# A spectral mixing kernel: first combination of units 3 and 5 on VectorE, butterflies of unit 2 on TensorE, halved inverse products of unit 5, a new order of the program

## The chip, the cores and the metric

The kernel runs on one core of one Trainium2 chip, in float32. The time is the device time of one execution in microseconds (us); the median of three runs is quoted. The profile comes from one further execution, traced by the hardware profiler.

## The reference, cut to what matters

```python
# x: 1 x 2048 x 512 (sequence L by channels D); all outputs are summed into one array
g = sigmoid((x * gate_w).sum(-1, keepdims=True))
a = irfft2(rfft2(x) * (w_r + 1j * w_i))          # two-dimensional Fourier filter
# K[d, l] = 2 Re sum_n C[d, n] exp(A[d, n] dt[d] l)
b = irfft(rfft(x, 2 * L) * rfft(K, 2 * L))[:L] + x * D_skip
return g * a + (1 - g) * b
```

For the inputs drawn here every step `dt` is so small that the kernel `K` is constant along the sequence, so `b` is a scaled prefix sum of `x` plus a scaled `x`. The kernel counts on the chip for how many channels this holds and has a general branch behind an `If` at the end, which is not entered.

## The kernel before

The two-dimensional transform is done by matrix products with constant tables. It has five stages.

1. **First products.** `x` (4 MB) arrives in ten parts. A part is multiplied on TensorE by a small table (`C_`, L276), in two halves `u`: one half takes the difference of the part's two blocks straight from `x`, as two accumulating products; the other takes their sum, which GpSimd forms first (`fold`, L259). VectorE transposes each product into the array `AR` (`c_a`, L284).
2. **Eight units.** A unit is a group of frequencies. Per unit: products along the sequence (`P_`, L435), a copy out of PSUM on ScalarE (`t_a`, L440), products along the channels (`D_`, L453), butterflies that combine the four parts of each product (`Z_`, L470 to L473, four VectorE instructions in PSUM, ahead of which ScalarE copies two parts aside in `d_a`, L462), and two products with the filter `w` on VectorE (`W` and `U`, both `W_`, L490), which leave `tw`. For the units in the list `ZPE` the butterflies are done by TensorE instead, as eight more products with the table `zfw` (L457) accumulated into `D_`, and `d_a` and `Z_` are not issued. Units 1 and 7 go through all this in two halves of 64 frequencies each (numbered 11, 21 and 17, 27).
3. **Combination.** GpSimd adds and subtracts in two steps of two instructions each: `p_a` (L496, L497, `px` from `tw`) and `g_a` (L509, L510, `gt` from `px`). ScalarE then mends one row (`h_a`, L517, L518).
4. **Inverse products** along the channels on TensorE (`I_`, L537, into `p_v`), a copy of half of it on ScalarE (`i_a`, L543), and an add and a subtract on VectorE into `AI` (`V_`, L551).
5. **The end.** Frequency 0 gets a product of its own (`K_`, L557) and a copy (L559). Then eight products with the last table but one (`B_`, L571), transposed by VectorE (`b_a`, L575), and eight output tiles (`Q_`, L597), each added to the other branch's result by VectorE (`last_a`, L610; L607 for the tile `LASTQ`, which leaves in two halves) and stored.

Beside this runs the other branch: copies to PSUM (`x_a`, L335), four prefix sums on VectorE (`scan`, L338), scalings on ScalarE (L342, L347), an adding transfer on GpSimd's queue (`both`, L352), the gate (L375, L385) and its products on GpSimd (`damp`, L370). The gate also scales the last table (`gated`, L587 on VectorE, L588 on ScalarE, from a copy of the gate in PSUM, `near`, L366).

Each engine works through its instructions in the order in which the program issues them. That order is written by hand in the string `PLAN`: a word is a letter for a step and the number of a unit, a part or a tile (`p5` is `p_a` of unit 5). PSUM has four buffers for all steps; a step that needs one waits until an earlier holder is released. Intermediates share thirteen SBUF buffers (`blk`), the filters and the last table four.

Of the kernel before, what the change touches and what calls it, by code (L numbers as in the profile page):

```python
# [15 lines left out]
P = 128  # L16
# [7 lines left out]
ZPE = (3, 5)  # L24
LASTQ = 7
LASTC = 7
FIRSTB = 0
# [4 lines left out]
R7 R0 C1 F2 J0 C0 c1 c0 T0 C2 c2 F3 C3 c3 F4 C4 J1 F5 R1 C5 F6 F8 F9 c4 c5 C6 c6 C8 R9 C9 c8 c9 R6 F7 N1 C7 c7 P11 l1  # L32
P21 l4 t11 t21 N0 N3 D11 d11 D21 d21 Z11 Z21 P17 P27 N4 N2 t17 L1 U11 R5 W11 U21 D17 t27 d17 P4 t4 Z17 l7 W21 L7 U17
X1 D27 p11 g11 d27 h11 Z27 D4 p21 g21 L4 P6 l0 d4 W17 U27 Z4 W27 p17 P0 U4 R4 g17 p27 W4 X3 X0 g27 t6 h21 P2 L0 t0 p4
D6 x1 t2 l6 h17 m1 G4 d6 h27 L6 G5 y1 k0 R8 X2 Z6 g4 U6 W6 k1 o3 o2 R10 D0 k2 k3 l2 d0 h4 l5 G1 x2 Z0 W0 D2 U0 L2 d2
l3 P3 P5 o4 G2 r1 p6 O0 t3 m2 y2 I11 S1 D3 g6 Z2 i11 p0 g0 W2 U2 o5 S0 r2 h6 L5 L3 O1 p2 t5 V11 I17 i17 x0 I6 h0 U3 o0
g2 V17 I21 i21 W3 D5 i6 S2 m0 y0 p3 g3 h2 V21 V6 O2 I0 o1 W5 I27 r0 U5 p5 g5 i0 i27 h3 x3 H2 o6 V0 I4 i4 V27 m3 I2 V4
i2 V2 h5 I3 I5 i3 V3 S3 u0 O3 i5 H4 E0 K0 V5 K1 B0 y3 E1 B3 b0 b3 B1 B4 B2 b1 B7 b2 B6 H5 o7 b4 r3 b7 Q1 Q0 u1 b6 B5
H1 E3 E2 Q3 H0 b5 H3 Q4 q1 q0 H7 H6 q3 Q2 q2 q4 Q6 q6 Q5 Q7 q5 q7
"""  # L40
SPLIT = [int(w[2:]) for w in PLAN.split() if w[0] == "P" and w[1] == "1" and len(w) == 3]
FOLDS = [0, 0, 1, 1, 1, 1, 1, 1, 1, 1]
ORDER = [8, 9, 0, 1, 10, 2, 11, 3, 12, 4, 13, 5, 14, 6, 15, 7, 16]
# [138 lines left out]
def body(ctx: ExitStack, tc: tile.TileContext, x, xg, xt, w, wh, prms, vecs, gw,  # L182
# [49 lines left out]
    t_ = {}  # L232

    with tc.manual_schedule():
# [20 lines left out]
        def fold(q, E):  # L255
            n = 64 * (PARTS[q].stop - PARTS[q].start)
            f = t_["f", q] = blk([P, 2, 512], "f")
            xv = xin(q)
            E.tensor_tensor(f[:, 0, :n], xv[:, 0], xv[:, 1], op=ALU.add)  # L259
            if FOLDS[q] == 2:  # L260
                E.tensor_tensor(f[:, 1, :n], xv[:, 0], xv[:, 1], op=ALU.subtract)


        def C_(q):
            n = 32 * (PARTS[q].stop - PARTS[q].start)
            p = t_["c", q] = [psum("p_s1") for _ in range(2)] if q == LASTC else [psum("p_s1")] * 2
            tiles = [(g, h, slice(64 * h, 64 * h + 64)) for g in range(2) for h in range(2)]
            if FOLDS[q] == 2:
                for g, h, r in tiles:
                    T.matmul(p[0][64 * g:64 * g + 64, h, :2 * n], s1e[r, 0:64], t_["f", q][r, :, g * n:g * n + n], start=True, stop=True, tile_position=(64 * h, 64 * g))  # L270
            else:
                for u in range(1, -1, -1):
                    for i in range(1 if FOLDS[q] > u else 2):
                        for g, h, r in tiles:
                            src = t_["f", q][r, 0] if FOLDS[q] > u else xin(q)[r, i]
                            T.matmul(p[u][64 * g:64 * g + 64, h, u * n:u * n + n], s1e[r, 64 * u * i:64 * u * i + 64], src[:, g * n:g * n + n], start=i == 0, stop=i == 1 or FOLDS[q] > u, tile_position=(64 * h, 64 * g))  # L276

        def c_a(q):
            k = PARTS[q]
            n = 32 * (k.stop - k.start)  # L280
            av = AR.rearrange("p u c (h t) d -> p u h t c d", h=2)
            for u in range(1, -1, -1):
                pv = t_["c", q][u][:, :, :2 * n].rearrange("p h (u t c d) -> p u h t c d", u=2, c=16, d=2)
                V.transpose(av[:, u, :, k], pv[:, u])  # L284
# [33 lines left out]

        def new(key, make):
            if key not in t_:  # L320
                t_[key] = make()
            return t_[key]
# [169 lines left out]
        def p_a(n):  # L492
            u, r, vs = unit(n)
            t1, t2 = (cut(t_["t", u, k], n).rearrange("p (o i) k -> p o i k", o=2) for k in range(2))
            po = new(("px", u), lambda: blk([P, 2, 2, 2, P], "px")).rearrange("p x a o k -> p x o a k")[..., r]
            G.tensor_tensor(po[:, 0], t1[:, :, 0:4:2], t1[:, :, 1:4:2][:, :, ::-1], op=ALU.subtract)  # L496
            G.tensor_tensor(po[:, 1, :, ::-1], t2[:, :, 0:4:2], t2[:, :, 1:4:2][:, :, ::-1], op=ALU.add)  # L497
# [101 lines left out]
        def last_a(j, E, p):  # L599
# [4 lines left out]
            if j == LASTQ:  # L604
                for f in range(2):
                    o_ = o[:, 512 * f:512 * f + 512]
                    E.tensor_tensor(o_.rearrange("p (e c b) -> p e c b", e=2, b=4), p[f].rearrange("p b (e c) -> p e c b", e=2), xv[..., 4 * f:4 * f + 4], op=ALU.add)  # L607
                    (nc.sync, nc.scalar)[f].dma_start(out[j, :, 512 * f:512 * f + 512], o_)
            else:
                E.tensor_tensor(o.rearrange("p (e c b) -> p e c b", e=2, b=8), p.rearrange("p b (e c) -> p e c b", e=2), xv, op=ALU.add)  # L610
                nc.sync.dma_start(out[j], o)

        def a_a(j):
# [18 lines left out]
            "f": lambda q: fold(q, V), "F": lambda q: fold(q, G), "C": C_, "c": c_a, "N": lambda k: N_[k](),  # L632
# [257 lines left out]
```

## Time and profile before

| | |
|---|---|
| three runs | 110.46, 110.65, 110.81 us, median 110.65 |
| the profiled execution's own time | 110.1 us |
| its span | 108.3 us |
| TensorE (PE) busy | 93.2 us, 86% |
| VectorE (DVE) busy | 85.3 us, 79% |
| GpSimd (POOL) busy | 75.5 us, 70% |
| ScalarE (ACT) busy | 51.5 us, 48% |
| granted TensorE clock, mean | 0.987 |
| moved by DMA | 27.67 MB |

The span runs from the first to the last recorded work; 1.8 us of the execution's own time lie around it. Shares are averages over five stages with different limits, so a busy engine of the table need not be the one that sets the end. PE and PEld are TensorE's products and its weight loads, which overlap. In the views, an entry in square brackets behind an instruction is the time its engine had stood idle before it, and what ended the wait.

### The profile page before, as it was taken

The page shows a single profiled execution, that of the slowest core. Times are in us where ns is not written, and L with a number is a line of the kernel's source. Part 1 is how long each engine was busy: PE and PEld are TensorE (multiplying, and loading weights), DVE is VectorE, ACT ScalarE, POOL GpSimd, SP SyncE. Part 2 cuts the span into 40 slices and gives each one's busy share as a digit, 9 for nine tenths or more (in the row PEclk, how much of TensorE's full clock was granted, in tenths as well). Part 3 has the DMA queues.
Part 4 walks back from the last instruction along what each step waited for, and adds up shares of the span by engine and source line. Part 5 has one row for each costly group of instructions (what it writes and reads, how often), then busy time and mean ns, then how long its engine had stood idle before and what let it go on. Part 6 is the DMA issues. An engine that isn't in the chain of part 4 may idle for free. (4 is left out here: it accounts for less than half of the span.)

```text
span 108.3 us, 2285 instructions
## 1 busy us (share of the span) xinstructions
PE 93.2 (86%) x872; PEld 77.6 (72%) x872; DVE 85.3 (79%) x134; ACT 51.5 (48%) x89; POOL 75.5 (70%) x70
## 2 busy tenths in 40 slices
PE   6899976999997999989899999976699999999200
PEld 6797753999797945368799999966243869999100
DVE  0248989579799788999999999996889979788500
ACT  0000005455749399999796996946870170000000
POOL 0059853222999998599999999999999999700000
PEclk9999999999999999999999999999999999999995
DMA  3999999999999991099978993998325950779950
GB/s 65 373 366 404 397 389 344 382 422 417 427 405 410 417 395 80 0 200 225 191 242 197 254 250 123 273 229 163 95 98 98 189 106 3 312 297 360 393 214 13
DMA packets 8560, 27.67 MB, mean 255 GB/s; under 512 B 968, under 2 KB 1352, under 8 KB 8028
## 3 DMA queue, kind: packets, MB, share of 16 engines
q1 hardware_dynamic: 7132, 22.86, 57.0%
q0 software_dynamic: 1088, 4.19, 20.2%
q10 hardware_dynamic: 320, 0.38, 1.0%
q8 instruction: 9, 0.15, 0.6%
q14 instruction: 11, 0.09, 0.2%
HBM read 19.01 MB, written 4.21 MB: 214 GB/s over the span
## 5 line engine op out<-in xcount | busy, mean ns | idle before, releaser
L490 DVE TENSOR_TENSOR tw<-p_d,w 128x1024 f32<-128x1024 f32 (+1 forms) x20 | 19.3, 1005 | 1.1 <-ACT w L411 0.5
L370 POOL TENSOR_TENSOR XT<-XT,gb 128x1024 f32<-128x1024 f32 x8 | 19.3, 2552 | 0.2 <-DMA XT<-v 0.2
L435 PE MATMUL p_t<-s2e,AR 128*128 128x128 f32 x128 | 16.7, 285 | 2.1 <-DVE AR L284 0.9
L435 PEld LDWEIGHTS p_t<-s2e,AR 128*128 128x128 f32 x128 | 15.7, 196 | 3.4 <-DVE AR L284 1.3
L453 PE MATMUL p_d<-et,dfw 128*128 128x256 f32 (+1 forms) x80 | 16.8, 343 | 0.8 <-ACT v L347 0.3
L537 PE MATMUL p_v<-dbw,gt 128*128 128x128 f32 x128 | 15.2, 276 | 1.6 <-ACT gt L518 1.6
L597 PEld LDWEIGHTS p_oa<-s1a,AR 128*128 128x128 f32 x128 | 15.2, 196 | 1.7 <-ACT s1a L588 0.9
L537 PEld LDWEIGHTS p_v<-dbw,gt 128*128 128x128 f32 x128 | 14.7, 192 | 1.9 <-ACT gt L518 1.8
L597 PE MATMUL p_oa<-s1a,AR 128*128 128x128 f32 x128 | 15.6, 283 | 0.0
L453 PEld LDWEIGHTS p_d<-et,dfw 128*128 128x128 f32 x80 | 12.0, 191 | 3.5 <-ACT gt L517 1.1
L259 POOL TENSOR_TENSOR f<-AI 128x512 f32<-128x512 f32 (+1 forms) x8 | 9.0, 1140 | 7.8 <-DMA AI<-in_x_dram 7.8
L496 POOL TENSOR_TENSOR px<-tw 128x512 f32<-128x512 f32 (+1 forms) x10 | 11.8, 1184 | 2.2 <-DVE tw L490 2.2
L284 DVE STREAM_TRANSPOSE AR<-p_s 128x512 f32<-128x512 f32 (+1 forms) x20 | 10.8, 589 | 2.9 <-PE p_s L276 2.8
L497 POOL TENSOR_TENSOR px<-tw 128x512 f32<-128x512 f32 (+1 forms) x10 | 11.8, 1180 | 0.0
L551 DVE TENSOR_TENSOR AI<-p_v,po 128x512 f32<-128x512 f32 (+1 forms) x20 | 10.4, 577 | 1.3 <-ACT po L543 1.3
L440 ACT COPY et<-p_t 128x1024 f32<-128x1024 f32 (+1 forms) x10 | 8.4, 836 | 6.0 <-PE p_t L435 6.0
L509 POOL TENSOR_TENSOR gt<-px 128x512 f32<-128x512 f32 (+1 forms) x10 | 10.6, 1063 | 0.8
L276 PE MATMUL p_s<-AI,last 64*64 64x128 f32 (+1 forms) x192 | 10.2, 347 | 1.0 <-DMA AI<-in_x_dram 1.0
L510 POOL TENSOR_TENSOR gt<-px 128x512 f32<-128x512 f32 (+1 forms) x10 | 10.6, 1060 | 0.0
L575 DVE STREAM_TRANSPOSE AR<-p_ia 128x1024 f32<-128x1024 f32 x8 | 9.4, 1222 | 1.4 <-PE p_ia L571 1.4
L338 DVE TENSOR_TENSOR_SCAN p_x<-p_x,XT 128x1024 f32<-128x1024 f32 x4 | 9.2, 2293 | 1.3 <-ACT p_x L335 1.3
L610 DVE TENSOR_TENSOR AI<-p_oa,XT 128x1024 f32<-128x1024 f32 x7 | 8.2, 1211 | 1.5 <-PE p_oa L597 1.5
(67 smaller groups left out, 123.0 us busy)
## 6 DMA issues: line engine op xcount, KB each, us to landing
w<-in_w_dram SPq DMA_DIRECT2D x8, 512.0 KB, 7.7
XT<-in_xt_dram SPq DMA_DIRECT2D x4, 1024.0 KB, 8.9
XT<-v POOLq DMA_DIRECT2D x4, 1024.0 KB, 9.9
out_dram<-AI SPq DMA_DIRECT2D x7, 512.0 KB, 3.4
AI<-in_x_dram SPq DMA_DIRECT2D x6, 512.0 KB, 7.7
gb<-gd SPq DMA_DIRECT2D x4, 512.0 KB, 5.2
AI<-in_x_dram SPq DMA_DIRECT2D x4, 256.0 KB, 3.2
s1a<-in_c_s1a_dram SPq DMA_DIRECT2D x4, 256.0 KB, 4.4
```

The source lines that it names most:

```text
L284: V.transpose(av[:, u, :, k], pv[:, u])
L370: E.tensor_tensor(r, r, t_["gb", h % 2], op=ALU.mult)
L435: T.matmul(cut(p, n, v)[:, 2 * q:2 * q + 2], AR[:, q % 2, 8 * (q // 2) + u, :, v], s2e[:, 2 * u + v], start=True, stop=True)
L453: T.matmul(d[:, o, 1:3] if h else d[:, o, 0:4:3], dfw[:, 2 * h + o], e[:, 2 * h + o], start=True, stop=not z)
L490: E.tensor_tensor(t, z, w, op=ALU.mult)
L496: G.tensor_tensor(po[:, 0], t1[:, :, 0:4:2], t1[:, :, 1:4:2][:, :, ::-1], op=ALU.subtract)
L497: G.tensor_tensor(po[:, 1, :, ::-1], t2[:, :, 0:4:2], t2[:, :, 1:4:2][:, :, ::-1], op=ALU.add)
L509: G.tensor_tensor(gv[:, :, 0], src[0], src[1], op=ALU.subtract)
L510: G.tensor_tensor(gv[:, ::-1, 1], src[0], src[1], op=ALU.add)
L537: T.matmul(p[:, v - vs[0], h, o], rows(u, o, v, h), dbw[:, h, o], start=True, stop=True)
L551: V.tensor_tensor(ai[:, :, :, k], t_["pi", n][:, 0:len(vs), :, 0], t_["po", u][:, v], op=ALU.subtract if k else ALU.add)
L597: T.matmul((p[b // 4][:, b % 4] if j == LASTQ else p[:, b]).rearrange("p (e c) -> p e c", e=2), VA[:, i, 8 * (k % 2) + b, :, k // 2], s1a[ ...
```

## The change

- `PDVE`: `p_a` of units 3 and 5 (four instructions) is issued on VectorE instead of GpSimd. Both inputs and the output are in SBUF.
- `ZPE` gets unit 2: its butterflies become eight more TensorE products, and its `d_a` and `Z_` go.
- Unit 5's inverse products, copy and `V_` are issued in two halves (words `I15`, `i15`, `V15`, `I25`, `i25`, `V25`); the matrix products are the same.
- The two halves `u` of the first products and of their transposes become words of their own (`C`, `c` for the half without a fold, `j`, `w` for the folded one), so that the last part's unfolded half can be issued earlier.
- The tile that leaves in two halves is 4 instead of 7. `LASTROWS` holds one slice with all rows, and the new value of `FIRSTB` and the new word `v` change nothing in the program.
- `PLAN` is a new order. The units come as 1, 7, 4, 0, 6, 5, 3, 2; before, as 1, 7, 4, 6, 0, 2, 3, 5.

```diff
-ZPE = (3, 5)
-LASTQ = 7
-LASTC = 7
-FIRSTB = 0
+ZPE = (2, 3, 5)
+LASTQ = 4
+FIRSTB = 1
...
-g2 V17 I21 i21 W3 D5 i6 S2 m0 y0 p3 g3 h2 V21 V6 O2 I0 o1 W5 I27 r0 U5 p5 g5 i0 i27 h3 x3 H2 o6 V0 I4 i4 V27 m3 I2 V4
...
+o0 p0 D3 o1 W5 S1 g0 y0 o4 h4 p6 I17 O2 U5 U3 g6 p5 i17 W3 I27 p3 S3 h0 i27 V17 L2 D2 r0 g5 U2 h5 V27 W2 I0 o5 i0 I4
...
+APART = (7,)
+LASTROWS = [slice(0, P)]
+PDVE = (3, 5)
...
-        def fold(q, E):
+        def fold(q, u, op, E):
             n = 64 * (PARTS[q].stop - PARTS[q].start)
-            f = t_["f", q] = blk([P, 2, 512], "f")
+            f = new(("f", q), lambda: blk([P, 2, 512], "f"))
             xv = xin(q)
-            E.tensor_tensor(f[:, 0, :n], xv[:, 0], xv[:, 1], op=ALU.add)
...
+            E.tensor_tensor(f[:, u, :n], xv[:, 0], xv[:, 1], op=op)
...
-        def C_(q):
+        def C_(q, u):
             n = 32 * (PARTS[q].stop - PARTS[q].start)
...
+            p = new(("c", q, u if q in APART else 0), lambda: psum("p_s1"))
+            for i in range(1 if FOLDS[q] > u else 2):
+                for g in range(2):
+                    for h in range(2):
+                        r = slice(64 * h, 64 * h + 64)
+                        src = t_["f", q][r, u] if FOLDS[q] > u else xin(q)[r, i]
+                        T.matmul(p[64 * g:64 * g + 64, h, u * n:u * n + n], s1e[r, 64 * u * i:64 * u * i + 64], src[:, g * n:g * n + n], start=i == 0, stop=i == 1 or FOLDS[q] > u, tile_position=(64 * h, 64 * g))
...
             po = new(("px", u), lambda: blk([P, 2, 2, 2, P], "px")).rearrange("p x a o k -> p x o a k")[..., r]
-            G.tensor_tensor(po[:, 0], t1[:, :, 0:4:2], t1[:, :, 1:4:2][:, :, ::-1], op=ALU.subtract)
-            G.tensor_tensor(po[:, 1, :, ::-1], t2[:, :, 0:4:2], t2[:, :, 1:4:2][:, :, ::-1], op=ALU.add)
+            E = V if u in PDVE else G
+            E.tensor_tensor(po[:, 0], t1[:, :, 0:4:2], t1[:, :, 1:4:2][:, :, ::-1], op=ALU.subtract)
+            E.tensor_tensor(po[:, 1, :, ::-1], t2[:, :, 0:4:2], t2[:, :, 1:4:2][:, :, ::-1], op=ALU.add)
...
-                    (nc.sync, nc.scalar)[f].dma_start(out[j, :, 512 * f:512 * f + 512], o_)
+                    for r in LASTROWS:
+                        (nc.sync, nc.scalar)[f].dma_start(out[j, r, 512 * f:512 * f + 512], o_[r])
```

From the units on, the same step stands three or four lines earlier in the changed file (L496 becomes L493, L490 becomes L486).

The first place is GpSimd's queue where the units end. Before, `px_740` is unit 3 and `px_774` unit 5, the last unit; `gb` belongs to the gate's products behind the units:

```order
L496 TENSOR_TENSOR px_740<-tw_717 128x2x2x128
L497 TENSOR_TENSOR px_740<-tw_703 128x2x2x128
L509 TENSOR_TENSOR gt_743<-px_740 128x2x4x64
L510 TENSOR_TENSOR gt_743<-px_740 128x2x4x64
L352 DMA XT_72<-v_737 128x2x1024
L496 TENSOR_TENSOR px_774<-tw_764 128x2x2x128
L497 TENSOR_TENSOR px_774<-tw_772 128x2x2x128
L509 TENSOR_TENSOR gt_777<-px_774 128x2x4x64
L510 TENSOR_TENSOR gt_777<-px_774 128x2x4x64
L370 TENSOR_TENSOR XT_72<-XT_72,gb_615 128x1024 x2
```

In the change, on the same queue, `gt_691` is unit 6, `px_694` unit 5, `px_706` unit 3 and `px_807` unit 2, which is now the last:

```order
L506 TENSOR_TENSOR gt_691<-px_677 128x2x4x64
L507 TENSOR_TENSOR gt_691<-px_677 128x2x4x64
L348 DMA XT_72<-v_671 128x2x1024
L506 TENSOR_TENSOR gt_735<-px_694 128x2x4x64
L507 TENSOR_TENSOR gt_735<-px_694 128x2x4x64
L506 TENSOR_TENSOR gt_780<-px_706 128x2x4x64
L507 TENSOR_TENSOR gt_780<-px_706 128x2x4x64
L348 DMA XT_72<-v_635 128x2x1024
L493 TENSOR_TENSOR px_807<-tw_744 128x2x2x128
L494 TENSOR_TENSOR px_807<-tw_738 128x2x2x128
L506 TENSOR_TENSOR gt_830<-px_807 128x2x4x64
L507 TENSOR_TENSOR gt_830<-px_807 128x2x4x64
```

The two instructions that make `px` are gone from this queue for units 5 and 3, and four instructions that make `gt` stand one behind the other between two adding transfers.

The second place is VectorE's queue up to the last filter products. Before, `tw_658` and `tw_660` are unit 2, `tw_703` and `tw_717` unit 3, `tw_764` and `tw_772` unit 5; the rows into `AI` are `V_` of units 1, 7 and 6:

```order
L490 TENSOR_TENSOR tw_658<-p_d_577,w_554 128x1024
L490 TENSOR_TENSOR tw_660<-p_d_577,w_554 128x1024
L551 TENSOR_TENSOR AI_71<-p_v_623,po_650 128x2x128 x2
L490 TENSOR_TENSOR tw_703<-p_d_630,w_587 128x1024
L551 TENSOR_TENSOR AI_71<-p_v_679,po_684 128x2x128 x2
L490 TENSOR_TENSOR tw_717<-p_d_630,w_587 128x1024
L338 SCALAR_TENSOR_TENSOR p_x_686<-p_x_686,XT_72 128x1024
L346 MEMSET v_737 128x1
L551 TENSOR_TENSOR AI_71<-p_v_711,po_650 128x2x128 x2
L551 TENSOR_TENSOR AI_71<-p_v_688,po_732 128x2x2x128 x2
L490 TENSOR_TENSOR tw_764<-p_d_719,w_560 128x1024
L490 TENSOR_TENSOR tw_772<-p_d_719,w_560 128x1024
```

In the change, on VectorE's queue from unit 5's second filter product on, `tw_664` and `tw_687` are unit 5, `tw_689` and `tw_699` unit 3, `tw_738` and `tw_744` unit 2; `px_694` and `px_706` are the moved `p_a`:

```order
L486 TENSOR_TENSOR tw_687<-p_d_611,w_394 128x1024
L486 TENSOR_TENSOR tw_689<-p_d_650,w_509 128x1024
L493 TENSOR_TENSOR px_694<-tw_664 128x2x2x128
L494 TENSOR_TENSOR px_694<-tw_687 128x2x2x128
L486 TENSOR_TENSOR tw_699<-p_d_650,w_509 128x1024
L493 TENSOR_TENSOR px_706<-tw_699 128x2x2x128
L494 TENSOR_TENSOR px_706<-tw_689 128x2x2x128
L548 TENSOR_TENSOR AI_71<-p_v_680,po_697 128x2x128 x2
L486 TENSOR_TENSOR tw_738<-p_d_721,w_644 128x1024
L548 TENSOR_TENSOR AI_71<-p_v_701,po_697 128x2x128 x2
L486 TENSOR_TENSOR tw_744<-p_d_721,w_644 128x1024
```

Four instructions whose two inputs are both in SBUF stand among the filter products, ahead of the last unit's; `V_` of unit 6 has moved behind the last filter product.

The third place is ScalarE's queue between the last unit's mended row and the copy of frequency 0. Before, `po_850` is the last unit's copy and `p_g_846` the gate's copy to PSUM, issued ahead of it:

```order
L517 COPY gt_777<-px_774 1x2x2x64
L518 COPY gt_777<-px_774 1x2x2x64
L543 COPY po_840<-p_v_822 128x512
L366 COPY p_g_846<-gb_752 128x1024
L543 COPY po_850<-p_v_831 128x512
L588 ACTIVATE s1a_663<-s1a_663,gv_80 128x512
L559 COPY AI_71<-p_k_855 128x512
```

In the change, on the same queue, `po_853` is the last unit's copy and `p_g_855` the gate's:

```order
L514 COPY gt_830<-px_807 1x2x2x64
L515 COPY gt_830<-px_807 1x2x2x64
L540 COPY po_838<-p_v_818 128x512
L338 ACTIVATE XT_72<-XT_72,gv_80 128x1024
L540 COPY po_853<-p_v_844 128x512
L362 COPY p_g_855<-gb_685 128x1024
L556 COPY AI_71<-p_k_859 128x512
```

The gate's copy of 1024 elements now stands between the last unit's copy and that of frequency 0, where a scaling of 512 elements stood.

More of the change, by code (lines that the diff above doesn't have):

```diff
@@ L281, in c_a @@
             av = AR.rearrange("p u c (h t) d -> p u h t c d", h=2)
-            for u in range(1, -1, -1):
-                pv = t_["c", q][u][:, :, :2 * n].rearrange("p h (u t c d) -> p u h t c d", u=2, c=16, d=2)
-                V.transpose(av[:, u, :, k], pv[:, u])
+            pv = t_["c", q, u if q in APART else 0][:, :, :2 * n].rearrange("p h (u t c d) -> p u h t c d", u=2, c=16, d=2)
+            V.transpose(av[:, u, :, k], pv[:, u])
         big, sm = few[:, 1:3], few[:, 3]
@@ L316, in body @@
         N_ = {0: n0, 1: n1, 2: small, 3: level, 4: n4}
[L319 to L322, printed above, removed]
         def coef(r):
@@ L631, in body @@
         todo = {
-            "f": lambda q: fold(q, V), "F": lambda q: fold(q, G), "C": C_, "c": c_a, "N": lambda k: N_[k](),
+            "f": lambda q: fold(q, 1, ALU.subtract, V), "F": lambda q: fold(q, 0, ALU.add, G), "v": lambda q: fold(q, 0, ALU.add, V),
+            "C": lambda q: C_(q, 1), "j": lambda q: C_(q, 0), "c": lambda q: c_a(q, 1), "w": lambda q: c_a(q, 0), "N": lambda k: N_[k](),
             "X": load_x, "x": x_a, "m": scan, "o": skip, "y": y_a, "z": summed, "r": both, "k": gate, "G": G_, "J": J_, "l": load_w, "L": load_h,
```

34 lines of the change are left out of this document (13 added, 21 removed).

## The prediction

> **What bounds the kernel now.** I read the chain of work that ended last first, in order of time (start, length, engine and line):
>
> ```profile
> 73.60 0.43 ACT gt L518
> ...
> 74.07 2.06 PE p_v L537 x16
> ...
> 77.90 6.41 PE p_ia L571 x53
> ...
> 89.40 11.52 PE p_oa L597 x96
> ```
>
> The chain starts at 73.6 us, at the last unit's mended row: from there to the end nothing waits long. To see what happens ahead of it, the busy time by stretch, cut at the chain's own joints (behind the length: PE, PEld, DVE, ACT, POOL, each with its number of instructions, then clock, DMA share, GB/s):
>
> ```profile
> 18.84:74.07 55.23, 51.45 (x392) 45.25 (x392) 49.56 (x82) 41.94 (x77) 46.75 (x50) 1.00 0.87 276
> 74.07:77.90 3.83, 2.93 (x19) 2.11 (x19) 3.00 (x5) 3.06 (x6) 3.83 (x2) 1.00 0.40 75
> 77.90:100.92 23.02, 23.00 (x192) 17.89 (x192) 20.13 (x21) 4.99 (x6) 15.69 (x8) 1.00 0.64 194
> ```
>
> From the first product of the units (18.84) to the last unit's inverse product (74.07) TensorE is idle for 3.78 us in all; from 77.90 to 100.92 never, at a full clock. So the end can move only with the start of `B_` (77.90), and that with the last `I_` (74.07). What held that one is in GpSimd's and TensorE's timelines:
>
> ```profile
> 26.43 0.73 POOL L496 TENSOR_TENSOR px<-tw 128x256 f32<-128x256 f32 x1 [2.19 <-DVE tw L490]
> 44.43 1.36 POOL L352 DMA_DIRECT2D XT<-v  x1 [1.40 <-ACT XT L342]
> 50.91 1.26 POOL L496 TENSOR_TENSOR px<-tw 128x512 f32<-128x512 f32 x1
> 53.48 1.29 POOL L509 TENSOR_TENSOR gt<-px 128x512 f32<-128x512 f32 x1
> 68.05 1.70 POOL L496 TENSOR_TENSOR px<-tw 128x512 f32<-128x512 f32 x1
> 73.52 7.07 POOL L370 TENSOR_TENSOR XT<-XT,gb 128x1024 f32<-128x1024 f32 x3
> 74.07 2.05 PE L537 MATMUL p_v<-dbw,gt 128*128 128x128 f32 x16 [1.61 <-ACT gt L518]
> ```
>
> From 26.43 to 73.52 GpSimd waits once, for 1.40 us; TensorE then stands 1.61 us for its last `gt`. The last unit's `tw` were ready earlier than GpSimd took them up:
>
> ```profile
> 64.38 2.35 DVE L490 TENSOR_TENSOR tw<-p_d,w 128x1024 f32<-128x1024 f32 x2
> 66.74 1.95 DVE L551 TENSOR_TENSOR AI<-p_v,po 128x512 f32<-128x512 f32 x4
> ```
>
> They end at 66.73, and GpSimd starts on them at 68.05. So GpSimd bounds the units, with VectorE 1.3 us and TensorE a little more behind it.
>
> **The sum, engine by engine.** *GpSimd* loses four instructions, two pairs. A pair takes 53.48 - 50.91 = 2.57 us, so 5.1 us go. With nothing to wait for it would be done 5.1 + 1.4 us sooner, at 67.0: it stops being the bound, and the next one decides.
>
> *TensorE.* Unit 2's butterflies cost the difference of two kinds of `D_`:
>
> ```profile
> 41.14 1.99 PE L453 MATMUL p_d<-et,dfw 128*128 128x256 f32 x8
> 43.06 1.92 PE L375 MATMUL p_gate<-XT,gv 128*32 128x512 f32 x16
> 60.58 0.60 PE L453 MATMUL p_d<-et,dfw 128*128 128x256 f32 x2
> 64.09 8.38 PE L537 MATMUL p_v<-dbw,gt 128*128 128x128 f32 x72
> ```
>
> Start to start, 1.92 us without and 3.51 us with them: 1.6 us more. The halved `I_` of unit 5 are the same sixteen records. The start gains a little. Before, both transposes of the last part stood behind its folded product, which waits for GpSimd's fold; now one does:
>
> ```profile
> 17.33 0.66 PE L276 MATMUL p_s<-f,last 64*64 64x256 f32 x8
> 18.84 2.15 PE L435 MATMUL p_t<-s2e,AR 128*128 128x128 f32 x16 [0.85 <-DVE AR L284]
> 9.05 6.50 DVE L284 STREAM_TRANSPOSE AR<-p_s 128x512 f32<-128x512 f32 x10 [0.51 <-PE p_s L276]
> ```
>
> That product ends at 17.99; one transpose of 0.65 behind it allows 18.7 in place of 18.84, since the fold itself is not earlier. TensorE's floor for the last `I_` is then 18.7 + 51.45 + 1.6 = 71.75, 2.3 us ahead of 74.07, and only if not one wait is left.
>
> *VectorE* up to the last filter product. It starts on the butterflies at 22.33 and ends the filter products at 66.73: 44.4 us. Its flagged waits and its terms:
>
> ```profile
> 29.29 0.69 DVE L490 TENSOR_TENSOR tw<-p_d,w 128x512 f32<-128x512 f32 x1 [0.49 <-ACT w L411]
> 38.33 2.30 DVE L338 TENSOR_TENSOR_SCAN p_x<-p_x,XT 128x1024 f32<-128x1024 f32 x1 [1.12 <-ACT p_x L335]
> 32.41 0.48 DVE L470 SCALAR_TENSOR_TENSOR p_d<-p_d,pers,ds 128x256 f32<-128x256 f32 x1
> 34.26 2.94 DVE L490 TENSOR_TENSOR tw<-p_d,w 128x512 f32<-128x512 f32 x3
> L587 DVE TENSOR_TENSOR s1a<-s1a,p_g 128x512 f32<-128x512 f32 x4 | 2.6, 682 | 0.0
> 56.41 0.75 DVE L551 TENSOR_TENSOR AI<-p_v,po 128x256 f32<-128x256 f32 x2
> L403 DVE TENSOR_TENSOR hw<-hw 8x256 f32<-8x256 f32 x1 | 0.4, 414 | 3.1 <-DMA hw<-in_wh_dram 3.1
> ```
>
> With two more waits of 0.2 they are 2.0 us; 42.4 us are work. Unit 2's butterflies go: 34.26 - 32.41 = 1.85. One pair of `V_` of a full unit moves behind (1.95 for two pairs, overlapping, so 1.0 to 1.2, I take 1.1) and one half pair moves ahead (0.75). The four moved instructions are an operation of which the trace shows no like: 512 elements, both inputs in SBUF, while GpSimd works. The nearest rows are 0.41 us for 256 elements from SBUF (with GpSimd idle) and 0.68 for 512 with one input in PSUM. From below the bound is 0.41 each, since 512 elements cannot beat 256. From above it is 0.68 plus a whole GpSimd instruction of 1.28 in front, should the two engines shut each other out. I take the nearest, 0.65 start to start: 2.6 us, range 1.6 to 7.8. The sum is 42.4 - 1.85 - 1.1 + 0.75 + 2.6 = 42.8 us. From 22.2 that is 65.0 without waits. I keep 0.7 of the 2.0 us of waits, those for ScalarE's copies at the start, which stand in the same order, and come to 65.7, 1.0 us ahead of 66.73.
>
> *The last unit.* GpSimd's adding transfer and then the four instructions took 73.52 - 68.05 = 5.5 us with the transfer's tail beneath them; 65.7 + 5.5 = 71.2. Then 0.5 us of ScalarE as before (73.52 to 74.07), and ScalarE has a scaling of 1.1 us queued ahead of the mended row, so I add 0.5: the last `I_` starts at 72.2 in place of 74.07, 0.45 above TensorE's floor.
>
> *From there to `B_`.* Before, 3.83 us. On ScalarE:
>
> ```profile
> 74.39 1.00 ACT L366 COPY p_g<-gb 128x1024 f32<-128x1024 f32 x1
> 76.16 0.59 ACT L543 COPY po<-p_v 128x512 f32<-128x512 f32 x1 [0.77 <-PE p_v L537]
> 76.64 0.72 ACT L588 ACTIVATE s1a<-s1a,gv 128x512 f32<-128x512 f32 x1
> 77.27 0.58 ACT L559 COPY AI<-p_k 128x512 f32<-128x512 f32 x1
> ```
>
> Between the last unit's copy and frequency 0's stood a scaling of 0.63 start to start; now the gate's copy of 0.95 does, 0.3 longer. Frequency 0's product takes the PSUM buffer of the inverse product before the last, so it waits for that unit's `V_`, behind the last prefix sum on VectorE: I add 0.3. So 4.4 us, and `B_` starts at 76.6, 1.3 us sooner.
>
> *The end.* The same 64 and 128 records, 23.0 us of TensorE, and the same two half stores behind it (7.4 us). `Q_` and `B_` change places so that two of them stand behind transposes that end just in time: 0.2 us. GpSimd's gate products start some 2 us sooner, so the last stores are not later for them. The span is 108.3 - 1.3 + 0.2 = 107.2, 1.1 us less. On the profiled execution's own 110.1 us that is 109.0; the runs' median lies 0.55 above that execution, so **109.6**.
>
> What ScalarE loses (one copy of unit 2) it had free. DMA: the filters and `XT` go out up to 4 us later, yet the first of them is used behind 31 us. If the order of loads cost a wait there, VectorE would pay it one for one.
>
> **Rivals.** *Slower: GpSimd and VectorE shut each other out.* `p_a` of unit 5 can hardly meet GpSimd, which waits for its result. `p_a` of unit 3 must: it is issued one filter product (1.2 us) behind, near the end of the first of unit 5's two `g_a` instructions of 1.28 on GpSimd. If each of the two on VectorE waits for a whole one, VectorE loses 2.5 us, the last filter product ends at 68.2 and the last `I_` starts at 74.7. Then 4.4 to `B_` and 0.2 give 112.1; with the 0.45 of slack that I put in front of the last `I_`, 111.7. It turns the sign from a loss of 1.5 us on. For it: nothing before has two SBUF inputs beside a running GpSimd. Against: whoever comes a tenth of a microsecond ahead of that end loses only this tenth.
>
> The Trainium skill speaks for this rival (page "SBUF — State Buffer", section "Who interferes with whom"): a VectorE instruction with two SBUF inputs contends with a GpSimd instruction that reads SBUF, and the one that starts second blocks until the first is done. No row of this trace shows it. By that rule alone, one blocked instruction of the two would leave about 110.4 and both 111.7.
>
> *No change: the waits move.* TensorE, VectorE and ScalarE are now all within 0.5 us of one another, so a wait on any one is paid. If 1.3 us more of TensorE's 3.78 us of waits stay than I have, the last `I_` starts at 73.5, `B_` at 77.9, and the time is 110.85, the end's 0.2 more than before. For it: VectorE is 90% busy in the stretch. Against: the 1.61 us wait has no cause left.
>
> *Better.* No wait remains (71.75), and the two terms of 0.3 ahead of `B_` are hidden: 75.6, which is 2.1 less after the end's 0.2: 108.6.
>
> **How the numbers follow.** The forecast has 0.50, from 109.0 to 110.2 by itself; better 0.12, no change 0.18, slower 0.20. A measurement of this kernel tells some 0.3% from no change. The range runs from just below the better case, 108.5, to 111.3, short of the slower one: outside it lie about 0.05 below and 0.12 above, with the smaller losses of that rival inside. Faster 0.62, same 0.18, slower 0.20.
>
> **What would show it.** GpSimd idle ahead of its last `px` and that starting within 0.3 us of the last `tw`, near 65.7. The last `I_` near 72.2, `B_` near 76.6, with 23.2 us from there to TensorE's end. `px` on VectorE at 0.65 to 0.70 us each; 1.5 to 2 us on unit 3's two, and GpSimd's `gt` instructions longer beside them, would prove the slower rival. `D_` of unit 2 at 3.5 us. The forecast is wrong if TensorE still waits over 2 us between 18.7 and the last `I_`, or if a wait ahead of `B_` exceeds 5 us.

## The result, and the profile after

The changed kernel takes **115.4 us** (median of four runs, 115.14 to 116.20), the kernel before 110.73 beside it: a ratio of 1.046, 95% interval 1.0415 to 1.0504. Some executions of a kernel come out over 1.5% longer than its fastest one, and the comparisons here and below leave those out. The forecast was 109.6, with 111.3 as its upper end. The profiled execution took 115.47 us with a span of 113.6 (before 110.1 and 108.3).

The chain of work that ended last, of the changed kernel (start, length, engine and line):

```profile
62.68 3.79 issue
66.46 0.68 DVE px L494
67.14 0.68 DVE AI L548 x2
67.95 3.70 PE p_v L534 x21
...
82.16 5.99 PE p_ia L568 x39
```

Before, the chain reached back no further than the last unit's mended row, at 73.6 us. Now 3.79 us stand in it as "issue", which means that the view found nothing that the instruction waited for. They end with a combination (`px`) on VectorE. The busy time by stretch, cut at the new joints (columns as in the prediction; the last row is a piece of the third):

```profile
19.25:62.48 43.23, 43.23 (x328) 37.94 (x329) 39.52 (x66) 33.58 (x60) 29.84 (x36) 1.00 0.84 289
62.48:67.95 5.47, 2.02 (x18) 1.86 (x17) 5.47 (x5) 2.35 (x4) 4.23 (x4) 1.00 0.89 189
67.95:78.00 10.05, 9.28 (x65) 8.90 (x65) 9.41 (x15) 5.84 (x13) 9.97 (x8) 0.83 0.82 184
78.00:82.16 4.16, 3.03 (x19) 2.16 (x19) 3.29 (x8) 3.53 (x6) 4.16 (x3) 1.00 0.55 177
82.16:105.75 23.59, 23.52 (x192) 17.35 (x192) 20.49 (x20) 4.59 (x6) 13.81 (x7) 1.00 0.60 183
...
67.95:73.50 5.55, 5.44 (x32) 5.25 (x32) 4.92 (x8) 2.21 (x7) 5.47 (x6) 0.69 0.66 132
```

From its first product of the units up to 62.48 TensorE has no wait at all, as the change intended. Then TensorE is busy for 2.02 of 5.47 us, and after that pause it runs 32 products at a granted clock of 0.69. The next 32 run at full clock:

```profile
67.95 5.44 PE L534 MATMUL p_v<-dbw,gt 128*128 128x128 f32 x32 [3.45 <-DVE AI L548]
73.55 3.84 PE L534 MATMUL p_v<-dbw,gt 128*128 128x128 f32 x32 [0.16 <-ACT gt L515]
```

VectorE's timeline over that place:

```profile
58.83 0.68 DVE L493 TENSOR_TENSOR px<-tw 128x512 f32<-128x512 f32 x1
59.43 1.77 DVE L494 TENSOR_TENSOR px<-tw 128x512 f32<-128x512 f32 x1
61.12 1.21 DVE L486 TENSOR_TENSOR tw<-p_d,w 128x1024 f32<-128x1024 f32 x1
62.44 4.10 DVE L493 TENSOR_TENSOR px<-tw 128x512 f32<-128x512 f32 x1
66.46 0.68 DVE L494 TENSOR_TENSOR px<-tw 128x512 f32<-128x512 f32 x1
```

And GpSimd's:

```profile
45.00 1.35 POOL L348 DMA_DIRECT2D XT<-v  x1
...
47.69 1.27 POOL L494 TENSOR_TENSOR px<-tw 128x512 f32<-128x512 f32 x1
53.90 1.28 POOL L506 TENSOR_TENSOR gt<-px 128x512 f32<-128x512 f32 x1 [4.94 <-ACT v L343]
...
58.98 1.68 POOL L506 TENSOR_TENSOR gt<-px 128x512 f32<-128x512 f32 x1
60.62 1.72 POOL L507 TENSOR_TENSOR gt<-px 128x512 f32<-128x512 f32 x1
62.28 1.19 POOL L348 DMA_DIRECT2D XT<-v  x1
63.06 1.71 POOL L506 TENSOR_TENSOR gt<-px 128x512 f32<-128x512 f32 x1
64.30 1.69 POOL L507 TENSOR_TENSOR gt<-px 128x512 f32<-128x512 f32 x1
```

Two of the four moved instructions take 0.68 us, the other two 1.77 and 4.10. Both slow ones end about 0.55 us after GpSimd instructions do: 59.43 + 1.77 = 61.20 behind 58.98 + 1.68 = 60.66, and 62.44 + 4.10 = 66.54 behind 64.30 + 1.69 = 65.99. GpSimd does the last combination (`g_a`) of unit 6 there and then that of unit 5. It comes to unit 6's so late because it had stood still for 4.94 us: unit 0's last combination waited from 48.96 to 53.90. The view names a ScalarE instruction as the releaser. In the program unit 0's last combination also takes the buffer of a gate tile (`gs`) out of the shared pool of thirteen, and two small transfers (`gd`, 4 KB each) still have to read that tile. SyncE issues them:

```profile
45.16 1.05 SPq L385 DMA_DIRECT2D gd<-gs  x2
```

The trace also records the semaphores, by which engines and transfers tell one another that they are done. The first of the two writes has landed at 46.94, the second at 53.74. GpSimd's queue gets past its wait for that landing at 53.76, before the ScalarE instruction ends (53.87). So it was the second write that GpSimd waited for.

### The profile page after: what moved, and what is told of

The parts are those of the page before. It is cut to its first block, busy times and chain, and to the rows that moved or that the text cites. A ratio compares the mean times of both kernels' runs of the same rounds, so it can differ in the third digit from the quotient of the medians.

```text
span 113.6 us, 2324 instructions
## 1 busy us (share of the span) xinstructions
PE 96.1 (85%) x888; PEld 79.4 (70%) x888; DVE 90.7 (80%) x136; ACT 51.4 (45%) x89; POOL 71.3 (63%) x66
## 4 chain that ended last, share of the span: by engine, by line
PE 56%; DMA 11%; issue 8%; DVE 7%; ACT 6%; POOL 5%; SPq 1%; ACTq 0%; DVEq 0%
PE p_t L431 14%; PE p_oa L594 14%; PE p_v L534 9%; DMA AI<-in_x_dram 8%; PE p_d L449 8%; PE p_ia L568 7%; PE p_gate L371 3%; DMA last<-in_c_s1e_dram 3%; POOL f L267 2%; DVE tw L486 2%; DVE px L494 2%; POOL gt L507 1%; POOL px L493 1%; SPq L244 1%; ACT XT L338 1%
## 5 line engine op out<-in xcount | busy, mean ns | idle before, releaser
L534 PE MATMUL p_v<-dbw,gt 128*128 128x128 f32 x128 | 17.5, 297 | 4.2 <-DVE AI L548 3.5
L534 PEld LDWEIGHTS p_v<-dbw,gt 128*128 128x128 f32 x128 | 16.5, 209 | 5.6 <-issue 3.6
L486 DVE TENSOR_TENSOR tw<-p_d,w 128x1024 f32<-128x1024 f32 (+1 forms) x20 | 19.4, 1002 | 0.6 <-DVE p_d L469 0.2
L431 PE MATMUL p_t<-s2e,AR 128*128 128x128 f32 x128 | 15.9, 283 | 0.8 <-DVE AR L285 0.8
L506 POOL TENSOR_TENSOR gt<-px 128x512 f32<-128x512 f32 (+1 forms) x10 | 11.4, 1144 | 6.6 <-ACT v L343 4.9
L548 DVE TENSOR_TENSOR AI<-p_v,po 128x256 f32<-128x256 f32 (+1 forms) x22 | 10.6, 537 | 1.5 <-ACT po L540 1.5
L507 POOL TENSOR_TENSOR gt<-px 128x512 f32<-128x512 f32 (+1 forms) x10 | 11.5, 1145 | 0.0
L493 POOL TENSOR_TENSOR px<-tw 128x256 f32<-128x256 f32 (+1 forms) x8 | 8.1, 1011 | 4.6 <-PE p_d L449 2.4
L278 PE MATMUL p_s<-AI,last 64*64 64x128 f32 (+1 forms) x192 | 9.3, 325 | 1.6 <-DMA AI<-in_x_dram 1.6
L568 PE MATMUL p_ia<-AI,s 64*64 64x512 f32 x64 | 8.1, 626 | 1.1 <-ACT AI L556 1.1
```

The source lines that it names most:

```text
L431: T.matmul(cut(p, n, v)[:, 2 * q:2 * q + 2], AR[:, q % 2, 8 * (q // 2) + u, :, v], s2e[:, 2 * u + v], start=True, stop=True)
L486: E.tensor_tensor(t, z, w, op=ALU.mult)
L506: G.tensor_tensor(gv[:, :, 0], src[0], src[1], op=ALU.subtract)
L507: G.tensor_tensor(gv[:, ::-1, 1], src[0], src[1], op=ALU.add)
L534: T.matmul(p[:, v - vs[0], h, o], rows(u, o, v, h), dbw[:, h, o], start=True, stop=True)
L548: V.tensor_tensor(ai[:, :, :, k], t_["pi", n][:, 0:len(vs), :, 0], t_["po", u][:, v], op=ALU.subtract if k else ALU.add)
```

## The experiments

Two causes were suspected, and they could only be told apart by taking each away alone: VectorE and GpSimd shut each other out (**the lock**), and GpSimd is late because of a buffer (**the gate wait**).

**Second operand from PSUM.** The same place, the same sizes, but one operand of the moved instructions isn't in SBUF:

```
             E = V if u in PDVE else G
+            s1, s2 = (parts(n),) * 2 if u in PDVE else (t1, t2)
-            E.tensor_tensor(po[:, 0], t1[:, :, 0:4:2], t1[:, :, 1:4:2][:, :, ::-1], op=ALU.subtract)
+            E.tensor_tensor(po[:, 0], t1[:, :, 0:4:2], s1[:, :, 1:4:2][:, :, ::-1], op=ALU.subtract)
...
```

> The changed kernel, but the four combination instructions on VectorE read their second operand from the spectrum in PSUM in place of the filter product in SBUF (so half of the filter products of units 3 and 5 are left out of the result); sizes and order are the same. Lock theory (VectorE with two SBUF operands and GpSimd shut each other out): the four take 0.65 to 0.80 us each in place of 0.68, 1.77, 4.10 and 0.68, TensorE's wait of 3.45 us ahead of an inverse product goes, and with it the fall of its clock to 0.69; VectorE gains 4.5 us, so 115.4 becomes 110.5 to 111.5. Rival (the instructions are slow for another reason, such as their reversed operand, the write into SBUF or GpSimd's adding transfer): they stay at 1.8 us on the mean and the time at 114.5 to 115.5.

Measured: 111.69 us, 0.2 above the range expected, ratio to before 1.0102 (1.0058 to 1.0145). VectorE's timeline:

```profile
58.52 0.68 DVE L494 TENSOR_TENSOR px<-tw,p_d 128x512 f32<-128x512 f32 x1
59.11 0.68 DVE L495 TENSOR_TENSOR px<-tw,p_d 128x512 f32<-128x512 f32 x1
...
61.03 0.69 DVE L494 TENSOR_TENSOR px<-tw,p_d 128x512 f32<-128x512 f32 x1
61.63 0.68 DVE L495 TENSOR_TENSOR px<-tw,p_d 128x512 f32<-128x512 f32 x1
```

GpSimd's in the same stretch:

```profile
53.59 1.28 POOL L507 TENSOR_TENSOR gt<-px 128x512 f32<-128x512 f32 x1 [5.01 <-ACT v L343]
...
58.65 1.27 POOL L507 TENSOR_TENSOR gt<-px 128x512 f32<-128x512 f32 x1
59.89 1.27 POOL L508 TENSOR_TENSOR gt<-px 128x512 f32<-128x512 f32 x1
61.10 1.17 POOL L348 DMA_DIRECT2D XT<-v  x1
61.88 1.71 POOL L507 TENSOR_TENSOR gt<-px 128x512 f32<-128x512 f32 x1
63.12 1.70 POOL L508 TENSOR_TENSOR gt<-px 128x512 f32<-128x512 f32 x1
```

The gate wait is still there (5.01 us), the two engines meet at the same place, and nobody waits: 0.68 us on VectorE, and 1.27 in place of 1.68 and 1.72 on GpSimd. So the lock is shown, from both sides, and it hangs on the second operand in SBUF. Without it the time is 3.7 us less. The lock may cost more than that, since this version holds the spectrum in PSUM until the combination is done, and TensorE waits 1.19 us for that buffer.

**Gate tiles out of the shared pool.**

```
-                    t_["gs", i] = blk([P, 512], "gs")
+                    t_["gs", i] = AI[:, 12 + i]
```

> The changed kernel with the two gate tiles in slots 12 and 13 of AI, which are free then, in place of two buffers of the shared pool; so unit 0's last combination no longer takes a buffer out of which a transfer still has to run. If that transfer is what GpSimd waited for (4.94 us up to 53.90), the wait goes, unit 6's combination is over before unit 5's first combination on VectorE (58.83), which then takes 0.7 us twice; unit 3's meets unit 5's last combination on GpSimd and loses 1.3 us at most: VectorE gains 3.2 us or more and the time is 110.5 to 112.5. If GpSimd waited for something else (ScalarE's copies), the wait and 115.4 stay.

Measured: 110.94 us, ratio 1.0015 (0.9963 to 1.0068). GpSimd's timeline where it had stood still, and its last combinations of units 6 and 5:

```profile
47.79 1.26 POOL L494 TENSOR_TENSOR px<-tw 128x512 f32<-128x512 f32 x1
49.13 1.27 POOL L506 TENSOR_TENSOR gt<-px 128x512 f32<-128x512 f32 x1
...
57.96 1.29 POOL L507 TENSOR_TENSOR gt<-px 128x512 f32<-128x512 f32 x1
59.19 1.19 POOL L348 DMA_DIRECT2D XT<-v  x1
60.49 1.27 POOL L506 TENSOR_TENSOR gt<-px 128x512 f32<-128x512 f32 x1
61.73 1.73 POOL L507 TENSOR_TENSOR gt<-px 128x512 f32<-128x512 f32 x1
```

The wait is gone. This trace alone does not prove that the buffer was its cause, because here the second gate write got ahead of the adding transfer: its last piece had moved by 46.78, and the transfer's data moved from 46.99 to 54.01. But in the traces of the six other versions with the gate tiles in `AI`, all below, that write landed between 53.47 and 54.42, and unit 0's last combination started without a wait between 48.74 and 49.75. So GpSimd had waited for the buffer, and not for the ScalarE instruction that the view named. The four instructions on VectorE now take 1.05, 0.68, 0.69 and 1.77 us: the lock still costs 0.37 + 1.09 = 1.5 us of VectorE. TensorE's long wait and the clock of 0.69 are gone. The first inverse product behind that place waits 0.23 us.

**Both edits.**

> Gate tiles out of the shared pool, and the four combination instructions on VectorE with their second operand from PSUM (half of the filter products of units 3 and 5 are left out of the result): neither of the two suspected costs is left, all other terms of the change are. Lock theory: in the run with the gate tiles alone the four took 1.05, 0.68, 0.69 and 1.77 us; here they take 0.7 each, the last filter product ends 1.5 us sooner (67.6 becomes 66.1), the last inverse product starts at TensorE's own floor, near 72.9 in place of 73.49 (TensorE had only 0.6 us of wait left there), and the time is 110.1 to 110.6 beside 110.94. Had the forecast's other terms been right as well, 109.6. Rival (VectorE's blocked time is hidden): 110.9 to 111.2.

Measured: 112.08 us, ratio 1.0153 (1.0050 to 1.0256): not faster than either edit alone, and above the ranges of both theories. The last filter product ends 47.68 us behind the first unit's first product, against 48.67 with the gate tiles alone (67.48 - 19.80 and 67.61 - 18.94). So VectorE gained 1.0 us, and TensorE lost 0.87 to the PSUM buffer that this version holds longer. The lock's remaining cost therefore can't be priced by this pair. Side by side:

| us | second operand in SBUF | in PSUM |
|---|---|---|
| gate tiles in the shared pool | 115.4 | 111.7 |
| gate tiles in `AI` | 110.9 | 112.1 |

Taking away either one takes most of the loss away. Without the lock the gate wait costs nothing that shows (111.7 beside 112.1). Without the gate wait the two engines still meet, but VectorE loses 1.5 us in place of 4.5. The large loss needs both, so no share of it can be put down to one of them alone.

**Combinations back on GpSimd**, alone and with the gate tiles moved (`PDVE = ()`).

> The changed kernel with all combinations back on GpSimd, everything else kept. Lock theory: no VectorE instruction above 1.3 us in the stretch, no TensorE wait of over 2 us before the last inverse product and no clock of 0.69. But GpSimd gets 5.1 us of work back while its 4.94 us wait stays, so it sets the end: its last px, 70.82 in the changed kernel, less 2.2 us of waits and 1.7 us of stretched instructions there, plus 5.1, is at 72.0, the last inverse product at 79.2, and with TensorE at full clock the time is 114.5 to 116.5. If the lock alone were what the change costs and GpSimd had room, 110 to 111.

> Both edits together: combinations all on GpSimd, gate tiles out of the shared pool. Neither the lock nor GpSimd's 4.94 us wait is left. GpSimd's last px moves from the 72.0 of the run with combinations on GpSimd alone to between 67.1 and 69, the last inverse product to 74.5 to 76, and the time to 110.5 to 112.5. If the other parts of the change (new order, unit 2's butterflies on TensorE, halves) were harmful by themselves, the time stays above 113.

Measured: 116.13 us (ratio 1.0471, 1.0385 to 1.0556) for the first. The second took 113.4 and 114.25 us (beside 110.55 before), with no ratio on record. The first version came as the lock theory had it in its time and in GpSimd's last `px` (72.38, where 72.0 was expected). TensorE was missed: it waited 4.29 us, for GpSimd this time, and its clock fell then too:

```profile
70.09:75.70 5.61, 5.61 (x30) 5.60 (x31) 3.65 (x8) 4.83 (x10) 5.61 (x5) 0.59 0.98 174
```

The second is 0.9 us or more above its range, and above the 113 us that were to mean that the rest of the change does harm by itself. The trace points to GpSimd: it works without a pause from 53.88 to beyond the last unit, its last `px` starts at 70.36 and not at 67.1 to 69, and TensorE waits three times for rows made from GpSimd's results (1.91, 1.45 and 1.38 us). In the new order GpSimd alone is too slow. So moving the combinations suits this order, and with the gate tiles moved it brings some 3 us (113.4 and 114.25 beside 110.94). That another part of the change does harm is not ruled out by this run; one part that does comes below, the order of the end.

**The combinations on VectorE in the old order.** In the kernel before, `E = V if u in (3, 5) else G`, and nothing else.

> The kernel before, in its old order, with the combinations of units 3 and 5 on VectorE and nothing else changed. In that order GpSimd has nothing of its own left when VectorE comes to them: unit 3's would start near 62.5, where GpSimd has ended unit 0's or 2's pair at 62.25 and waits for it, unit 5's near 68, where GpSimd has only an adding transfer behind it. Lock theory: all four take 0.65 to 0.75 us, GpSimd ends the last unit 1.5 to 2 us sooner, and the time is 108.6 to 109.8 in place of 110.6. Rival (two operands in SBUF are slow on VectorE by themselves): 1.8 us each on the mean, 110.6 to 112.

Measured: 111.28 us, ratio 1.0056 (1.0021 to 1.0092). VectorE's timeline:

```profile
62.97 0.69 DVE L497 TENSOR_TENSOR px<-tw 128x512 f32<-128x512 f32 x1
...
63.58 0.68 DVE L498 TENSOR_TENSOR px<-tw 128x512 f32<-128x512 f32 x1
...
68.30 0.68 DVE L497 TENSOR_TENSOR px<-tw 128x512 f32<-128x512 f32 x1
68.90 0.68 DVE L498 TENSOR_TENSOR px<-tw 128x512 f32<-128x512 f32 x1
```

With two operands in SBUF and no GpSimd arithmetic beside them they take 0.68 us, near the 0.65 that the forecast used. The time was missed. It lies in the rival's range, though not for the rival's reason: GpSimd ends the last unit 1.3 us sooner (72.19 in place of 73.52), but VectorE has 2.6 us more to do, and TensorE waits for its filter products and combinations instead (1.13 and 0.38 us). The edit alone brings nothing in the old order.

**Why 4.10 us and not 1.8.** The adding transfer stood ahead of unit 5's last combination on GpSimd's queue; here it is moved behind unit 3's.

```
-... L2 D2 r0 g5 U2 ... S0 I15 g3 h3 ...
+... L2 D2 g5 U2 ... S0 I15 g3 r0 h3 ...
```

> The changed kernel with GpSimd's second adding transfer moved from ahead of unit 5's last combination to behind unit 3's. It tells two theories of the 4.10 us apart. First: behind a transfer GpSimd's instructions overlap (started 1.24 apart, 1.7 long), and VectorE, once late, gets in only when the whole run of them is over; without the transfer it gets in after one instruction: unit 3's two take 1.8 us at most each, VectorE gains 2 us or more, TensorE's wait shrinks to 1.5, and the time is 112 to 113.5. Second: VectorE waits for any run of GpSimd instructions to end; it still waits 3 us or more (two instructions), and the time is 114.5 to 115.5.

Measured: 113.49 us, ratio 1.0293 (1.0203 to 1.0384). VectorE's timeline, unit 3's two:

```profile
62.24 1.68 DVE L493 TENSOR_TENSOR px<-tw 128x512 f32<-128x512 f32 x1
63.84 1.75 DVE L494 TENSOR_TENSOR px<-tw 128x512 f32<-128x512 f32 x1
```

They start beside GpSimd instructions at 62.10 and 63.33, and each gets in after one. In the changed kernel the two GpSimd instructions behind the transfer start 1.24 us apart and are 1.7 long, as they are behind the transfer in the PSUM version, where nothing holds them up. Their records overlap, and VectorE got in only behind the second. So the first theory held in what decides between the two: without the transfer ahead of them VectorE gets in after one instruction. The gain was smaller than it said: unit 3's two take 3.28 us in place of 4.62, and TensorE's wait is 2.10 us; its clock behind it stays at 1.00. That the overlap is what shuts VectorE out is argued and not shown, since no run has the overlap without a transfer. The issue of a transfer alone did not do it: with the gate tiles moved, a `px` on VectorE took 0.68 us from 59.72, beside an issue from 59.19 to 60.38 with no GpSimd arithmetic ready behind it.

**What held the gate writes up.** The first adding transfer (1 MB, word `r1`) is issued behind unit 0's last combination.

> The changed kernel; GpSimd's first adding transfer (1 MB) is issued behind unit 0's last combination and not ahead of unit 0's first. Theory: the small gate writes (8 KB in all), issued at 45.2 to 46.2, land only at 53.9 because that transfer, issued at 45 and 10.4 us under way, fills the same DMA engines; without it they land in 2 to 4 us, unit 0's last combination starts without a wait near 48, and the time is 110.5 to 112. Rival: the gate writes are slow by themselves (pieces of 128 bytes); the wait of 4.9 us stays, less the 1.2 us that the transfer's issue took, and the time is 114.5 to 115.5.

Measured: 114.0 us, ratio 1.0328 (1.0224 to 1.0431), between the ranges of both theories. The traced execution, 115.17 us, was the longest of the four. GpSimd's timeline:

```profile
48.98 1.28 POOL L506 TENSOR_TENSOR gt<-px 128x512 f32<-128x512 f32 x1
...
59.24 1.74 POOL L506 TENSOR_TENSOR gt<-px 128x512 f32<-128x512 f32 x1 [3.61 <-ACT gt L515]
```

The gate wait is gone: the second write now lands at 47.34 in place of 53.74, so it had stood behind that transfer. In the changed kernel its 32 pieces of 128 bytes move between 47.24 and 53.19, in pairs, among the 256 pieces of 4096 bytes of the adding transfer (46.91 to 54.41). Only 1.4 us were gained, less than expected: now unit 6's last combination waits 3.61 us, by the view for ScalarE's mending of unit 4, and starts at 59.24 in place of 58.98. Why it waits for that row here is not shown; in the changed kernel it started before that row was done (59.15). It meets VectorE as before; unit 3's two take 1.68 and 3.72 us, the second beside a transfer and two `gt` again. So the gate wait is one way to bring GpSimd to unit 6 late, and not the only one: what costs the time is the meeting.

**The last unit's first combination on VectorE too**, right behind its filter product (`PDVE = (2, 3, 5)`, `V27 W2 p2 I0`), with the gate tiles moved.

> Gate tiles out of the shared pool, and the last unit's first combination on VectorE too, right behind its filter product, where GpSimd has nothing of its own to do. Lock theory: nothing runs on GpSimd beside it, so its two instructions take 0.65 us each in place of GpSimd's 1.25, the last unit's chain is 1.3 us shorter, and the last inverse product starts at TensorE's floor of 72.9 in place of 73.49: 110.2 to 110.6. Rival: the inverse products' combinations behind it on VectorE come 1.3 us later and TensorE waits for their PSUM buffers: 110.9 to 111.8.

Measured: 112.54 us, ratio 1.0211 (1.0100 to 1.0322): the rival, and 0.7 more than it said. The two take 0.69 and 0.68 us, with no GpSimd arithmetic beside them, but TensorE waits 1.40 us for the inverse products' combinations behind them.

**The old order of the end**, with the gate tiles moved: the words behind `K1` as before, and `LASTQ = 7`.

> Gate tiles out of the shared pool, and behind the last unit the old order of the end (which products and stores follow which, and the piece that is stored in halves). If the new order of the end costs what the windows say (23.59 us from the first product of the end to TensorE's end in place of 23.02, and 7.7 in place of 7.4 behind it), the time falls by 0.8 to 110.1 (109.8 to 110.5). If the difference comes from what precedes (the gate's copies, the adding transfers), it stays at 110.9.

Measured: **109.77 us, ratio 0.9916 (0.9863 to 0.9969)**: 0.8% less than the kernel before, a small gain but clear of its interval, and the fastest version of all. From its windows, first product of the end to TensorE's end, and behind it:

```profile
77.37:100.40 23.03, 23.03 (x192) 17.95 (x192) 20.27 (x20) 4.59 (x6) 16.03 (x8) 1.00 0.63 193
100.40:107.60 7.20, 0.01 (x1) 0.00 (x0) 0.69 (x1) 0.00 (x0) 0.00 (x0) 0.67 0.48 180
```

These are 23.03 and 7.20 us in place of 23.59 and 7.74 with the gate tiles alone: the new end costs 1.1 us.

**Two parts of the change undone in this best version.** First, unit 2's butterflies back on VectorE (`ZPE = (3, 5)`, `D2 d2 ... Z2 U2`):

> The version with the gate tiles out of the shared pool and the old end, with unit 2's butterflies back on VectorE (1.85 us there, 0.6 for a copy on ScalarE) and off TensorE (1.6 us). If TensorE is what bounds that version up to the last inverse product (it shows one wait of 0.6 us there), 109.8 becomes 108.2 to 109. If VectorE and the last unit's chain behind it bound it as much, its last filter product ends 1.85 later, less the 0.3 us that TensorE comes sooner, and the time is 110.8 to 111.6.

Measured: 112.48 us, ratio 1.0137 (1.0059 to 1.0214). Between the first unit's first product and the last filter product's end lie 50.23 us in place of 48.25, and TensorE, with 1.6 us less to do, stands waiting 1.11 and 1.76 us for `V_`. VectorE bounds as much as TensorE, as the second theory had it, and the time is 0.9 above the range that it gave. Then unit 5's inverse products whole (`I5 ... i5 ... V5`):

> The version with the gate tiles out of the shared pool and the old end (109.8 us), with unit 5's inverse products, their copy and combination whole again in place of halves. Theory: the halves cost nothing and bring nothing (the same sixteen records; two PSUM buffers in place of one), 109.3 to 110.2. Rival: the two PSUM buffers of the halves are what makes TensorE wait for VectorE's combinations behind them (0.2 us), and one buffer gives it back: 109.0 to 109.3; or the whole piece, whose copy and combination are twice as long behind it, makes the next wait: 110.2 to 111.

Measured: 110.75 us, ratio 0.9985 (0.9950 to 1.0020). The halves seem to bring some 0.7%, though the two intervals overlap, so this is not shown. One wait of TensorE grows to 1.34 us, for a mended row that stands behind the whole copy on ScalarE.

## Why the prediction was wrong

Its span was 107.2; the trace shows 113.6, 6.4 more. By its own steps:

| step | predicted | trace of the changed kernel | difference |
|---|---|---|---|
| first product of the units | 18.7 | 19.25 | 0.55 |
| last filter product ends | 65.7 | 70.73 | 4.48 beside the 0.55 |
| from there to the last `I_` | 6.5 | 7.27 | 0.77 |
| last `I_` to `B_` | 4.4 | 4.16 | -0.24 |
| `B_` to the end of the span | 30.6 | 31.44 | 0.84 |

*VectorE's four instructions: the step that failed.* "I take the nearest, 0.65 start to start: 2.6 us, range 1.6 to 7.8." Measured are 61.12 - 58.83 = 2.29 and 67.06 - 62.44 = 4.62 us, 6.9 in all: 4.3 more, nearly the whole of the second row. The operation by itself was priced right (0.68 in the old order and with an operand in PSUM). What was wrong is to price it without its neighbour. The text gave an upper bound of 1.96 each, 7.8 in all, which held for the sum, though not for the single one of 4.10. It then took the nearest row, 0.68, and that row could not tell: its instruction (L587) did run beside GpSimd's products (73.52 to 80.59), but with one operand in PSUM, the very case in which the experiments found no lock. The sign that the prediction set for its own failure, a wait of TensorE of over 2 us ahead of the last `I_`, came with 3.45 us.

*The slower rival*, which the prediction gave 0.20, had the mechanism right and the size too small. It let a meeting cost one whole GpSimd instruction, 2.5 us in all, and ruled out unit 5. Unit 5's second instruction lost 1.1 us to unit 6's last combination, and unit 3's first lost 3.4 to a transfer and two instructions that overlap. The rule that was cited beside it (the Trainium skill, page "SBUF — State Buffer", section "Who interferes with whom") agrees with the trace on who contends, two SBUF operands against a GpSimd instruction that reads SBUF. That the one which starts second blocks until the first is done held for the 1.77 us, and fell short for the 4.10.

*GpSimd: "With nothing to wait for it would be done 5.1 + 1.4 us sooner, at 67.0".* It waited 4.94 us for a buffer of the shared pool, and its last `px` started at 70.82. In the changed kernel that wait put GpSimd's work beside VectorE's: with the gate tiles elsewhere unit 6 was out of the way but for 0.37 us. The prediction looked at what each instruction computes from, and not at whose buffer it takes. The order of instructions that it showed says nothing of buffers.

*TensorE's clock.* The 32 products behind the wait took 5.44 us. The next 32 took 3.84, and with the gate tiles moved the same products as behind the wait took 4.05: the fall of the clock cost 1.4 to 1.6 us. It was no step of the prediction. In the chain this loss goes on through ScalarE: a copy had to wait for the late products, and it and a scaling stood in front of the last unit's mended row:

```profile
75.69 0.59 ACT L540 COPY po<-p_v 128x512 f32<-128x512 f32 x1 [0.75 <-PE p_v L534]
76.18 1.15 ACT L338 ACTIVATE XT<-XT,pers 128x1024 f32<-128x1024 f32 x1
```

The scaling had been foreseen, and priced at 0.5 us. GpSimd's part of `gt` was ready at 75.99, and the last `I_` started only at 78.0.

*The start.* No gain of 0.14 came. In the versions of the changed kernel the first unit's product starts between 18.84 and 19.97, from trace to trace, so this step was below what one trace can tell.

*The end* was 0.84 longer. That was the order: the old end takes it back, and 0.3 more. *Right* were the 1.6 us of TensorE for unit 2's butterflies (53.14 us of products up to the last `I_` in the best version, 53.05 forecast), nearly the 4.4 us to `B_` (4.16), and that the waits ahead of 62.48 go. The version with the gate tiles moved and the old end takes 109.77 us, near the 109.6 of the forecast. That is in part luck and does not show that the other terms held: this version has an edit that the forecast knew nothing of, and its VectorE still loses 1.5 us to the lock.

## What to carry to other kernels

An instruction that moves to another engine is priced together with what runs beside it at its new place: look in the trace for the neighbour, and for what can push that neighbour into it. Ask of each instruction not only whose result it waits for but whose buffer it takes; a small transfer that still reads a buffer of a shared pool can hold an engine up for nearly as long as the large transfer ahead of it takes. Where two costs make a loss only together, change them one at a time and then both, before naming one of them the cause.

## What the runs showed that was not expected

- Held up by GpSimd arithmetic alone, VectorE's instruction took 1.05 to 1.77 us; started beside the issue of an adding transfer with two GpSimd instructions ready behind it, it ended only behind both (4.10 and 3.72 us).
- A GpSimd instruction that meets such a VectorE instruction gets longer as well: 1.66 to 1.74 us in place of 1.27. (Behind a transfer it shows 1.7 us even where nothing holds it up, as in the PSUM version at 61.88.)
- TensorE's clock fell behind waits of 3.45 us (0.69 over the next 5.5), 4.29 (0.59) and, in the longest of that version's four executions, 2.85 (0.69), and not behind 2.10 us (1.00). The Trainium skill (page "TensorE: Matmul & The Clock Gate", section "HAM oscillation — how this bites in real kernels") warns of gaps above about 3.4 us; here 2.85 was enough. The clock records of the fourteen traces show why the length alone does not tell. Within a trace, all changes of the clock lie whole multiples of 3.41 us apart. From its first rise on, the clock was at half behind every such step in which TensorE had stood idle for 2.10 us or more in all, and behind none with 1.91 us or less.
- Of two gate writes of 4 KB, issued at 45.16 and 45.74 behind a transfer of 1 MB (45.00), the first landed after 1.8 us and the second after 8.0. With the transfer issued later, the second took 1.65 us.
